# Attention and routed experts on one core: lead rows written ahead of the last load, two tiles' rows side by side, and two groups' norms on GpSimd

## Chip, core and metric

The kernel runs on one core of one Trainium2 chip. The metric is the device time of one execution in microseconds (us); for the kernel before the median of three runs is 536.72 us (535.98 to 536.99). About 0.2%, or 1.07 us, is what a measurement of this kernel can tell from no change. The engines are TensorE (PE, with weight loads as PEld), VectorE (DVE), ScalarE (ACT), GpSimd (POOL) and SyncE (SP), which here only issues DMAs.

## What is computed

There are 8 batches of 576 tokens with 8 heads of 64. Linear attention gives each token a 512-wide row, each head's part is normed by its root mean square, and each token goes to the one of 8 experts that its gate picks.

```python
kv  = einsum('bhsd,bhse->bhde', k, v)
out = einsum('bhsd,bhde->bhse', q, kv)
rms = sqrt(mean(out * out, -1) + 1e-6);  x = out / rms * g_norm      # (4608, 512)
logits = x @ w_gate;  e_idx = argmax(logits, 1)
y[mask e] = prob(e_idx) * sigmoid(x @ w_output_gate)[e] * relu(x @ w1[e]) @ w2[e]
```

## The kernel before

**First part, the rows.** The 4608 tokens are 36 tiles of 128. SP loads 54 pieces of 512 KB (`load`, L705): 32 of k and v (`kvm`), 4 remainders (`rem`) and 18 of q (`qT`), each of the latter for two tiles. The list `loads` holds them in a fixed order, and the last entry is `qT` piece 17, for tiles 34 and 35. A load needs a free slot out of `SLOTS - ROWS` = 20. For each tile `out_tile` (L788) does the PE matmuls into a PSUM tile `ops`, `out_rows` (L815) lets ACT copy the row (`xrow`), its squares (`sq`) and its gate products (`gp`), and `sums` (L833) lets DVE add up the squares (`ss`). ACT follows PE by one tile, and DVE follows ACT by one.

**Groups.** The tiles form groups of 16, 10 and 10. When a group's last `ss` is there, `route` (L849) turns its sums into inverse norms `rv` (nine DVE instructions, L858 to L872), scales the gate products, picks the expert, counts tokens per expert through small PE matmuls (`rp`), and closes the rows (`C_SCALE`, by a reciprocal). `STEPS` says after which tile which step of which group is written; `TAIL` is the order behind tile 35: `Q` flushes rows and sums, a digit is one step of that group, `W` loads W2, `C` is 8 matmuls of constants that keep PE at work, `L` is one step of the lead run, and so on. Rows go to DRAM (`xs`), where row 1 + 128 t + p is token p of tile t.

**Lead run.** The first 16 tiles' rows (group 0) are enough for a lead run of 256 tokens of the largest expert. Its rows are written by five DMAs (`xs<-xrow`, 8 tiles in one and 2 in each of four) as soon as the group is closed and no load is left (L1038). GpSimd then gathers the 256 rows by index (`gather(0)`, hook `G` at tile 35), DVE scales them by `rv` (`scale_heads`, L283), PE transposes them (`tps`, L307) and goes on with the lead's matmuls (L338, L590). The writes of groups 1 and 2 follow, then `gather(1)` for the rest of that expert's tokens, whose transposes stand in the lead's last matmuls, and after that the run of experts one behind another.

All four compute engines and SP take their work in the order in which it stands, one queue each. `qT`, `kvm`, `xs` and weight DMAs of SP share one hardware queue.

```python
if not loads and not opened[0]:                        # L1038: rows of the lead
    nc.sync.dma_start(out=xs[0:1, :].rearrange("o (a x) -> (o a) x", x=16), in_=zrow)
    open_rows(0)
...
xwrite(c0, xs[1 + c0 * P:1 + (c0 + k) * P].rearrange("(t p) x -> p t x", p=P), x)
```

Of the kernel before, what the change touches and what calls it, by code (L numbers as in the profile page):

```python
# [21 lines left out]
P = 128  # L22
# [78 lines left out]
def constants(gn, wg):
    k = np.zeros((P, K_N), np.float32)
    m = np.arange(P)
    e = np.arange(E)
    k[:, K_E:K_E + E] = e
    k[:, K_ER:K_ER + E] = e * NTOK
    k[:, K_SC:K_SC + E] = E - e
    k[:, K_CAP:K_CAP + E] = CAP
    k[:, K_FL:K_FL + E] = [c // P for c in CAP]
    k[:, K_TRI:K_TRI + E * E] = (e[None, :] < e[:, None]).reshape(-1)  # L110
    k[:, K_M1] = m + 1
    g = np.arange(NT)
    k[:, K_G:K_G + NT] = g
    k[:, K_V:K_V + NT] = g[None, :] * P + m[:, None] + 1
# [22 lines left out]
def body(ctx: ExitStack, tc: tile.TileContext, kvm, rem, qT, w1, w2, kc, xs, tab, out):  # L137
# [511 lines left out]
    wgs = cf[:, K_WG:K_N].rearrange("q (i x) -> q i x", i=2)  # L649
# [198 lines left out]

    def route(gi):  # L849

        ss, gp, lg = gst[gi]
        n = len(GROUPS[gi])
        last = gi + 1 == len(GROUPS)
        g0 = GROUPS[gi][0]
        vec = nc.vector

        a = sm.tile([P, GMAX, E], F32, name="ra", bufs=1)[:, :n]
        vec.tensor_scalar(out=a, in0=ss[:, :n], scalar1=1.0 / D, scalar2=1e-6, op0=ALU.mult, op1=ALU.add)  # L858
        y = sm.tile([P, GMAX, E], F32, name="ry", bufs=1)[:, :n]
        vec.tensor_scalar(out=y.bitcast(I32), in0=a.bitcast(I32), scalar1=-0.5,  # L860
                          scalar2=float(0x5F3759DF), op0=ALU.mult, op1=ALU.add)
        u = sm.tile([P, GMAX, E], F32, name="ru", bufs=1)[:, :n]
        rv = sm.tile([P, GMAX, E], F32, name="rv")[:, :n]

        q = 0.375 ** 0.5
        vec.scalar_tensor_tensor(out=u, in0=y, scalar=q, in1=y, op0=ALU.mult, op1=ALU.mult)
        vec.tensor_tensor(out=u, in0=u, in1=a, op=ALU.mult)
        vec.scalar_tensor_tensor(out=u, in0=u, scalar=-1.25 / q, in1=u, op0=ALU.add, op1=ALU.mult)
        vec.scalar_tensor_tensor(out=y, in0=u, scalar=1.875, in1=y, op0=ALU.add, op1=ALU.mult)
        vec.scalar_tensor_tensor(out=u, in0=y, scalar=-0.5, in1=y, op0=ALU.mult, op1=ALU.mult)  # L870
        vec.tensor_tensor(out=u, in0=u, in1=a, op=ALU.mult)
        vec.scalar_tensor_tensor(out=rv, in0=u, scalar=1.5, in1=y, op0=ALU.add, op1=ALU.mult)  # L872
# [91 lines left out]
        for t in range(n):  # L964
# [8 lines left out]
        vec.tensor_scalar(out=rc[:, :n, 0], in0=rc[:, :n, 1], scalar1=cf[:, K_M1:K_M1 + 1], scalar2=None, op0=ALU.mult)  # L973
# [146 lines left out]
    def rows_of_lead(out):  # L1120
# [262 lines left out]
    with ExitStack() as p3:  # L1383
# [4 lines left out]
        with tc.If(nreg > 0):  # L1388
            with tc.For_i(0, nreg) as i:
# [13 lines left out]
                nc.vector.tensor_copy(gi, gf)  # L1403
# [81 lines left out]
```

## Time and profile before

| what | us |
|---|---|
| median of 3 runs | 536.72 |
| the profiled execution's own time | 536.44 |
| its span | 534.6 |
| PE busy in the span | 522.6 |
| DVE, ACT, POOL busy | 382.3, 295.8, 265.4 |

The span is what the profiler saw between the first and the last instruction, the time also has what lies around it, here 1.84 us. PE is busy in nearly all of the span, but a share of busy time over the whole says little on one place: some of PE's work is constants that fill a wait. So the stretch that the change touches is read row by row: what each engine did there, what it waited for, and when DMAs landed.

### The profile page before, as it was taken

Reading aid. Unit: us, or ns where it says so; the run is one execution under the profiler, and the core shown is the slowest. Engines: PE = TensorE matmul, PEld = TensorE weight load, DVE = VectorE, ACT = ScalarE, POOL = GpSimd, SP = SyncE. Lnnn points to the kernel's source line nnn. Section 1 sums busy time; section 2 is a strip of 40 time slices with the busy share of each in tenths; the row PEclk is TensorE's granted clock in tenths of the full one; section 3 lists DMA queues with packets and bytes.
Section 4 is the critical chain, followed back from the end, with each engine's and each line's share of the span. In section 5 each row is a group of like instructions: output and inputs, shape, how many; then the busy total and the mean of one; then the engine's idle time right before and its main releaser. Section 6 shows DMA issues by size and latency. Waiting matters only on the chain.

```text
span 534.6 us, 10844 instructions
## 1 busy us (share of the span) xinstructions
PE 522.6 (98%) x4047; PEld 455.5 (85%) x4047; DVE 382.3 (72%) x834; ACT 295.8 (55%) x603; POOL 265.4 (50%) x275
## 2 busy tenths in 40 slices
PE   9899997999999999999999999999999999999995
PEld 6789886857988998899889988998899889889984
DVE  2225999974599779666895699578868978897710
ACT  1568673333558638365655565556465657485611
POOL 1000243232885269607960696079807963894011
PEclk9999999999999999999999999999999999999999
DMA  8999999965205340616044603360436053415001
GB/s 315 416 417 417 413 400 360 374 229 180 86 30 188 108 155 20 221 59 214 21 140 133 212 21 140 131 195 35 143 126 198 30 201 123 142 44 195 2 31 40
DMA packets 28420, 92.27 MB, mean 173 GB/s; under 512 B 3758, under 2 KB 3886, under 8 KB 28365
## 3 DMA queue, kind: packets, MB, share of 16 engines
q1 hardware_dynamic: 22124, 71.85, 36.5%
q0 software_dynamic: 6240, 19.70, 11.3%
q8 instruction: 33, 0.54, 0.4%
q14 instruction: 23, 0.18, 0.1%
HBM read 72.34 MB, written 19.64 MB: 172 GB/s over the span
## 4 chain that ended last, share of the span: by engine, by line
PE 78%; DMA 11%; DVE 8%; issue 1%; ACT 1%; POOL 0%; SPq 0%; POOLq 0%; ACTq 0%; DVEq 0%
PE yps L609 35%; PE hpsa L494 17%; PE hpsd L494 9%; DMA ld<-kvm 5%; PE hps L494 4%; PE hps L359 4%; PE yps L603 3%; DMA xs<-xrow 2%; DMA ld<-qT 2%; DVE ss L837 2%; PE tps L460 2%; DMA xg<-xs,gidx 2%; DVE gp L882 1%; DVE lg L886 1%; PE ops L811 1%
## 5 line engine op out<-in xcount | busy, mean ns | idle before, releaser
L609 PE MATMUL yps<-whi,hT 128*128 128x512 f32 (+3 forms) x560 | 184.2, 395 | 0.0
L609 PEld LDWEIGHTS yps<-whi,hT 128*128 128x128 f32 (+3 forms) x560 | 104.0, 186 | 22.3
L609 PE MATMUL yps<-wlo,hT 128*128 128x512 f32 (+3 forms) x280 | 109.7, 392 | 0.0
L623 POOL DMA_INDIRECT out<-y,oidx x41 | 51.8, 1263 | 89.1 <-ACT y L622 60.9
L265 POOL DMA_INDIRECT xg<-xs,gidx x42 | 43.9, 1046 | 93.9 <-ACT hT L514 37.9
L609 PEld LDWEIGHTS yps<-wlo,hT 128*128 128x128 f32 (+3 forms) x280 | 52.1, 186 | 9.9
L517 DVE SCALAR_TENSOR_TENSOR hT<-ct,hT 128x256 fp32r<-128x256 f32 (+9 forms) x88 | 44.0, 529 | 22.8 <-ACT hT L514 22.8
L514 ACT ACTIVATE hT<-ct 128x328 fp32r<-128x328 f32 (+13 forms) x56 | 34.6, 617 | 34.1 <-DVE ct L528 34.1
L494 PE MATMUL hpsa<-xb,wh 128*128 128x328 f32 (+6 forms) x224 | 47.5, 300 | 0.0
L494 PE MATMUL hpsd<-xT,wh 128*128 128x328 f32 (+6 forms) x224 | 47.4, 299 | 0.0
L494 PE MATMUL hpsa<-xT,wh 128*128 128x328 f32 (+6 forms) x224 | 47.4, 299 | 0.0
L837 DVE TENSOR_REDUCE ss<-sq 128x8 f32<-128x512 f32 x36 | 23.7, 680 | 29.3 <-ACT sq L827 29.3
L419 DVE SCALAR_TENSOR_TENSOR wl<-wraw,cf,wh 128x512 fp32r<-128x512 f32 (+1 forms) x56 | 44.0, 824 | 0.2 <-ACT wh L418 0.2
L283 POOL TENSOR_TENSOR xg<-xg 128x512 f32<-128x512 f32 (+7 forms) x36 | 38.3, 1075 | 11.2 <-DVE ct L549 9.0
L228 DVE TENSOR_TENSOR wlo<-wraw,whi 128x1024 fp32r<-128x1024 f32 x32 | 39.8, 1243 | 5.7 <-ACT whi L225 5.2
L419 DVE SCALAR_TENSOR_TENSOR wl<-ws,cf,wh 128x1024 fp32r<-128x1024 f32 x28 | 42.9, 1532 | 0.0
L622 ACT ACTIVATE y<-yps,tl 128x512 f32<-128x512 f32 (+3 forms) x37 | 25.4, 687 | 31.2 <-PE yps L609 17.7
L811 PE MATMUL ops<-aug,ld 64*128 64x80 f32 (+1 forms) x640 | 38.9, 271 | 1.5 <-ACT gp L828 1.4
L418 ACT ACTIVATE wh<-ws,cf 128x1024 fp32r<-128x1024 f32 x28 | 32.4, 1156 | 13.3 <-POOL ws L405 13.3
L494 PEld LDWEIGHTS hpsd<-xT,wh 128*128 128x128 f32 x224 | 37.1, 188 | 1.3
L494 PEld LDWEIGHTS hpsa<-xT,wh 128*128 128x128 f32 x224 | 37.0, 188 | 1.4
L494 PEld LDWEIGHTS hpsa<-xb,wh 128*128 128x128 f32 x224 | 37.1, 188 | 1.3
(231 smaller groups left out, 1145.3 us busy)
## 6 DMA issues: line engine op xcount, KB each, us to landing
wraw<-w SPq DMA_DIRECT2D x64, 512.0 KB, 4.0
ld<-kvm SPq DMA_DIRECT2D x32, 512.0 KB, 10.0
ld<-qT SPq DMA_DIRECT2D x18, 512.0 KB, 10.3
xs<-xrow SPq DMA_DIRECT2D x9, 528.0 KB, 6.7
xs<-xrow SPq DMA_DIRECT2D x2, 1320.0 KB, 11.3
xs<-xrow SPq DMA_DIRECT2D x1, 2112.0 KB, 12.4
ld<-rem SPq DMA_DIRECT2D x4, 512.0 KB, 9.8
xg<-xs,gidx POOLq DMA_INDIRECT x42, 3.9
```

The source lines that it names most:

```text
L228: eng.tensor_tensor(out=lo, in0=r, in1=hi.bitcast(F32), op=ALU.subtract)
L265: gathered = nc.gpsimd.indirect_dma_start(out=x[:M, :], out_offset=None, in_=rows, in_offset=bass.IndirectOffsetOnAxis(ap=gidx[:M, p, t:t ...
L283: return eng.tensor_tensor(out=v, in0=v, in1=f, op=ALU.mult)
L418: nc.scalar.activation(hi, x, AF.Copy, scale=gcol[:, 0:1])
L419: nc.vector.scalar_tensor_tensor(out=lo, in0=x, scalar=gcol[:, 0:1], in1=hi.bitcast(F32), op0=ALU.mult, op1=ALU.subtract)
L494: nc.tensor.matmul(ps, W[a][d], X[b][d], start=start and k == 0, stop=k == 5, skip_group_check=not start)
L514: S.activation(hh, x, AF.Relu)
L517: V.scalar_tensor_tensor(out=v(o, j1 - j0), in0=x[..., j0:j1], scalar=0.0, in1=hh[..., j0:j1].bitcast(F32), op0=ALU.max, op1=ALU.subtract)
L609: nc.tensor.matmul(ps[:M], a, b, start=(f == 0 and j == 0), stop=(f == 7 and j == 2))
L623: i_ = nc.gpsimd.indirect_dma_start(out=out, out_offset=bass.IndirectOffsetOnAxis(ap=oidx[:M, p, t:t + 1], axis=0), in_=y[:M], in_offset=N ...
L811: nc.tensor.matmul(v[r0:r0 + m, u, p, :], qt[g // 2][r, p, q0:q0 + m], augs[b % 3][r, p, :], start=True, stop=True)
L837: nc.vector.tensor_reduce(out=o, in_=sq, axis=AX.X, op=ALU.add)
```

## The change

Four things are changed.

1. `HELD = 1`: the last load stays back. The lead's writes are issued when the group is closed (`lead_known`) and only one load is left; that load follows them. `ROWS` is 10 and no longer 9, so that 19 slots are left for loads, and group 2's rows lie in pieces of 4, 4 and 2 tiles and no longer 5 and 5.
2. Rows of tiles 2j and 2j+1 lie side by side in DRAM: partition p of a write is one run of 4224 bytes and no longer two of 2112. Row numbers change with it (`2 * P` for `P`, two constants for m + 1), and `scatter_rows` has to undo it with six instructions where there were two.
3. For groups 0 and 1 the inverse norm is made tile by tile on GpSimd, with two instructions of 8 columns (scale and add, then `pow` -0.5); the nine DVE instructions stay for group 2 alone.
4. `TAIL` has four `C` ahead of the first `L`, and no longer seven.

```diff
-ROWS = 9
+ROWS = 10
-BIG = {26: 5, 31: 5}
+BIG = {26: 4, 30: 4}
-TAIL = "Q112WCCCCCCCLcL2L2L22L2L1L12L1KAL2AL"
+TAIL = "Q112WCCCCLcL2L2L22L2L1L12L1KAL2AL"
+HELD = 1
+NORM_GROUPS = 2
-        while loads and free and n:
+        while loads and free and n and (opened[0] or len(loads) > HELD):
 def sums():
         nc.vector.tensor_reduce(out=o, in_=sq, axis=AX.X, op=ALU.add)
+        if r is not None:
+            nc.gpsimd.tensor_scalar(out=o, in0=o, scalar1=1.0 / D, scalar2=1e-6, op0=ALU.mult, op1=ALU.add)
+            nc.gpsimd.tensor_tensor(out=r, in0=o, in1=cf[:, K_MH:K_N].to_broadcast([P, E]), op=ALU.pow)
 def route(gi):
+        if gi >= NORM_GROUPS:
...
-            xwrite(c0, xs[1 + c0 * P:1 + (c0 + k) * P].rearrange("(t p) x -> p t x", p=P), x)
+            xwrite(c0, xs[1 + c0 * P:1 + (c0 + k) * P].rearrange("(j p u) x -> p j (u x)", p=P, u=2), x)
...
-            if not loads and not opened[0]:
+            if len(loads) <= HELD and lead_known and not opened[0]:
                 nc.sync.dma_start(out=xs[0:1, :].rearrange("o (a x) -> (o a) x", x=16), in_=zrow)
                 open_rows(0)
+                load()
 def scatter_rows(q0, q1, t0, t1):
-        vec.scalar_tensor_tensor(out=oidx[:, q0:q1, t0:t1], in0=f, scalar=-1.0, in1=zf, op0=ALU.add, op1=ALU.add)
...
+        vec.tensor_tensor(out=a, in0=a, in1=b, op=ALU.bitwise_or)
+        vec.tensor_scalar(out=r, in0=r, scalar1=0xFFFF00, scalar2=None, op0=ALU.bitwise_and)
+        vec.tensor_tensor(out=oidx[:, q0:q1, t0:t1], in0=r, in1=a, op=ALU.bitwise_or)
```

On SP's queue, at the end of the loads, this stood (`ld` is a load, `xs` the rows in DRAM, `wraw` a weight):

```order
L712 DMA ld<-kvm 128x1024 x2
L712 DMA ld<-qT 128x1024 x2
L1039 DMA xs<-zrow 33x16
L1001 DMA xs<-xrow_110 128x8x528
L1001 DMA xs<-xrow 128x2x528 x4
L189 TENSOR_LOAD epos
```

and this stands now:

```order
L720 DMA ld<-kvm 128x1024 x2
L720 DMA ld<-qT 128x1024
L1056 DMA xs<-zrow 33x16
L1017 DMA xs<-xrow_110 128x4x1056
L1017 DMA xs<-xrow 128x1056 x4
L720 DMA ld<-qT 128x1024
L197 TENSOR_LOAD epos
```

One of the two `qT` loads has moved behind the five writes, whose rows are now runs of 1056 numbers.

On PE, at the last four tiles (32 to 35, a tile's eight matmuls in two rows), with buffer numbers and waits, this stood:

```order
L811 MATMUL ops_1407<-aug1_104,ld_881 128x80 [waits DMAHW5_49,PE_49]
L811 MATMUL ops_1407<-aug1_104,ld_881 128x80 x7
L811 MATMUL ops_1421<-aug1_104,ld_881 128x80 [waits PE_49,Activation_49]
L811 MATMUL ops_1421<-aug1_104,ld_881 128x80 x7
L811 MATMUL ops_1435<-aug1_104,ld_907 128x80 [waits DMAHW6_49,PE_49,Activation_49]
L811 MATMUL ops_1435<-aug1_104,ld_907 128x80 x7
L811 MATMUL ops_1454<-aug1_104,ld_907 128x80 [waits PE_49,Activation_49]
L811 MATMUL ops_1454<-aug1_104,ld_907 128x80 x7
```

and this stands now:

```order
L820 MATMUL ops_1445<-aug1_104,ld_932 128x80 [waits DMAHW5_49,PE_49]
L820 MATMUL ops_1445<-aug1_104,ld_932 128x80 x7
L820 MATMUL ops_1459<-aug1_104,ld_932 128x80 [waits PE_49,Activation_49]
L820 MATMUL ops_1459<-aug1_104,ld_932 128x80 x7
L820 MATMUL ops_1473<-aug1_104,ld_1176 128x80 [waits DMAHW4_49,PE_49,Activation_49]
L820 MATMUL ops_1473<-aug1_104,ld_1176 128x80 x7
L820 MATMUL ops_1492<-aug1_104,ld_1176 128x80 [waits PE_49,Activation_49]
L820 MATMUL ops_1492<-aug1_104,ld_1176 128x80 x7
```

The order of PE is the same, but the load that tile 34 reads (`ld_907`, now `ld_1176`) is the one that has moved.

On DVE, behind the last sum of group 0, this stood:

```order
L858 TENSOR_SCALAR ra<-ss 128x128
L860 TENSOR_SCALAR ry<-ra 128x128
L866 SCALAR_TENSOR_TENSOR ru<-ry 128x128
L867 TENSOR_TENSOR ru<-ru,ra 128x128
L868 SCALAR_TENSOR_TENSOR ru<-ru 128x128
L869 SCALAR_TENSOR_TENSOR ry<-ru,ry 128x128
L870 SCALAR_TENSOR_TENSOR ru<-ry 128x128
L871 TENSOR_TENSOR ru<-ru,ra 128x128
L872 SCALAR_TENSOR_TENSOR rv<-ru,ry 128x128
L837 TENSOR_REDUCE ss<-sq 128x8
L882 TENSOR_TENSOR gp_311<-gp_311,rv 128x2048
```

and this stands now:

```order
L896 TENSOR_TENSOR gp_311<-gp_311,rv 128x2048
L846 TENSOR_REDUCE ss<-sq 128x8
L900 TENSOR_REDUCE lg<-gp_311 128x256
L907 TENSOR_REDUCE mx<-lg 128x16
L909 TENSOR_TENSOR rd<-lg,mx 128x128
```

The nine instructions of the norm are gone from DVE there, and from group 1 in the same way; group 2 keeps them.

## Rows read from the trace of the kernel before

**Rows 1.** Page, busy us, share of the span and instructions of each engine.
```profile
PE 522.6 (98%) x4047; PEld 455.5 (85%) x4047; DVE 382.3 (72%) x834; ACT 295.8 (55%) x603; POOL 265.4 (50%) x275
```

**Rows 2.** Chain that ended last, 30 to 150 us: start, us, what.
```profile
88.09 4.40 DMA xg<-xs,gidx
...
100.68 12.77 DMA xs<-xrow
...
114.38 4.00 DMA xg<-xs,gidx
...
119.15 0.65 PE tps L307 x4
```

**Rows 3.** Timeline of SP, 60 to 81 us: start, us of issuing, what, count.
```profile
63.38 0.33 SPq L712 DMA_DIRECT2D ld<-qT  x1
...
67.59 7.67 SPq L1001 DMA_DIRECT2D xs<-xrow  x5
...
74.10 1.16 SPq L1001 DMA_DIRECT2D xs<-xrow  x1
76.71 3.76 SPq L198 DMA_DIRECT2D wraw<-w  x4
```

**Rows 4.** DMAs issued at 63.38, 74.10 and 76.71: KB, us to landing.
```profile
ld<-qT SPq DMA_DIRECT2D x1, 512.0 KB, 11.0
...
xs<-xrow SPq DMA_DIRECT2D x1, 528.0 KB, 11.5
...
wraw<-w SPq DMA_DIRECT2D x1, 512.0 KB, 10.0
```

**Rows 5.** Stretches: length, PE, PEld, DVE, ACT, POOL busy; PEclk, DMA share, GB/s.
```profile
20.00:40.00 20.00, 19.16 (x392) 16.97 (x391) 6.18 (x10) 14.49 (x37) 0.00 (x0) 1.00 1.03 417
75.00:82.00 7.00, 5.84 (x120) 5.24 (x116) 6.74 (x16) 5.12 (x14) 2.01 (x5) 1.00 1.06 383
...
532.00:533.00 1.00, 0.00 (x0) 0.00 (x0) 0.00 (x0) 0.00 (x0) 0.00 (x0) 0.63 0.23 86
533.00:534.00 1.00, 0.00 (x0) 0.00 (x0) 0.00 (x0) 0.00 (x0) 0.00 (x0) 0.50 0.00 0
```

**Rows 6.** Timeline of PE: start, us, line, operation, count, idle before.
```profile
1.17 5.64 PE L719 MATMUL kvp<-ones 128*128 128x256 bf16 x26 [1.17 <-DVE ones L662]
...
78.04 2.91 PE L811 MATMUL ops<-aug,ld 64*128 64x80 f32 x48
82.34 1.12 PE L811 MATMUL ops<-aug,ld 64*128 64x80 f32 x16 [1.39 <-ACT gp L828]
...
86.82 4.53 PE L719 MATMUL cps<-ones 128*128 128x256 bf16 x40 [0.17 <-ACT gp L828]
92.44 0.63 PE L307 MATMUL tps<-ident,xg 128*128 128x128 f32 x4 [1.09 <-DVE tl L303]
...
528.91 0.39 PE L609 MATMUL yps<-whi,hT 128*128 128x512 f32 x1
```

**Rows 7.** Timeline of DVE, same columns.
```profile
49.52 0.23 DVE L858 TENSOR_SCALAR ra<-ss 128x128 f32<-128x128 f32 x1
...
52.00 0.29 DVE L872 SCALAR_TENSOR_TENSOR rv<-ru,ry 128x128 f32<-128x128 f32 x1
...
86.17 1.27 DVE L837 TENSOR_REDUCE ss<-sq 128x8 f32<-128x512 f32 x2
...
91.60 0.74 DVE L283 TENSOR_TENSOR xg<-xg 128x512 f32<-128x512 f32 x1 [0.24 <-DMA xg<-xs,gidx]
```

**Rows 8.** Timeline of ACT, same columns.
```profile
84.14 0.65 ACT L825 COPY xrow<-ops 128x512 f32<-128x512 f32 x1
...
85.32 0.67 ACT L825 COPY xrow<-ops 128x512 f32<-128x512 f32 x1
85.86 0.63 ACT L827 ACTIVATE sq<-ops 128x512 f32<-128x512 f32 x1
```

**Rows 9.** Timeline of POOL, same columns.
```profile
52.36 2.92 POOL L874 COPY xrow<-rv 128x64 f32<-128x64 f32 x5 [44.15 <-DVE rv L872]
```

More of the change, by code (lines that the diff above doesn't have):

```diff
@@ L91 @@
 K_M1 = K_TRI + E * E
-K_G = K_M1 + 1
+K_G = K_M1 + 3
 K_V = K_G + NT
-K_C = K_V + NT
+K_C = K_V + 2 * NT
 K_I = K_C + E * TMAX
@@ L97 @@
 K_WG = K_GN + 1
-K_N = K_WG + 8 * E
+K_MH = K_WG + 8 * E
+K_N = K_MH + 1
 def constants(gn, wg):
@@ L110, in constants @@
     k[:, K_TRI:K_TRI + E * E] = (e[None, :] < e[:, None]).reshape(-1)
-    k[:, K_M1] = m + 1
+    k[:, K_M1:K_M1 + 3] = np.stack([m + 1, 2 * m + 1, 2 * m + 2], 1)
     g = np.arange(NT)
-    k[:, K_G:K_G + NT] = g
-    k[:, K_V:K_V + NT] = g[None, :] * P + m[:, None] + 1
+    k[:, K_G:K_G + NT] = g // 2
+    k[:, K_V:K_V + 2 * NT:2] = g[None, :] * P + m[:, None] + 1
+    k[:, K_V + 1:K_V + 2 * NT:2] = g[None, :] // 2 * (2 * P) + 2 * m[:, None] + g[None, :] % 2 + 1
     k[:, K_C:K_C + E * TMAX] = ((e[:, None] * NT + np.arange(TMAX)) * P).reshape(-1)
@@ L117, in constants @@
     k[:, K_GN:K_GN + 1] = gn
-    k[:, K_WG:K_N] = wg
+    k[:, K_WG:K_MH] = wg
+    k[:, K_MH] = -0.5
     return k
@@ L156, in body @@
     meti = cst.tile([P, NOVER], I32, name="meti")
-    cst.tile([P, 56], F32, name="pad")
+    cst.tile([P, 48], F32, name="pad")
     main = ctx.enter_context(ExitStack())
@@ L794, in out_tile @@
                        sm.tile([P, max(GR[gi % 2::2]), 16, H], F32, name=f"gp{gi % 2}", bufs=1),
-                       sm.tile([P, GMAX, 16], F32, name="lg"))
+                       sm.tile([P, GMAX, 16], F32, name="lg"),
+                       sm.tile([P, GMAX, E], F32, name="rv"))
         ps = ps_b.tile([P, 2, 512], F32, name="ops", tag="big")
@@ L820, in out_rows @@
         gi, t, n = group_of(g)
-        ss, gp, lg = gst[gi]
+        ss, gp, lg, rv = gst[gi]
         c0, k, x = next(c for c in chunks if c[0] <= g < c[0] + c[1])
@@ L828, in out_rows @@
         nc.scalar.copy(gp[:, t].rearrange("q x (u p) -> q u p x", u=2), v[:, :, :, D:W])
-        squares.append((sq, ss[:, t, :], gi if t + 1 == n else None))
+        squares.append((sq, ss[:, t, :], rv[:, t, :] if gi < NORM_GROUPS else None, gi if t + 1 == n else None))
     outs = []
@@ L834, in sums @@
     def sums():
-        sq, o, gi = squares.pop(0)
+        sq, o, r, gi = squares.pop(0)
         nc.vector.tensor_reduce(out=o, in_=sq, axis=AX.X, op=ALU.add)
+        if r is not None:
+            nc.gpsimd.tensor_scalar(out=o, in0=o, scalar1=1.0 / D, scalar2=1e-6, op0=ALU.mult, op1=ALU.add)
+            nc.gpsimd.tensor_tensor(out=r, in0=o, in1=cf[:, K_MH:K_N].to_broadcast([P, E]), op=ALU.pow)
         if gi is not None:
@@ L849, in route @@
     def route(gi):
-        ss, gp, lg = gst[gi]
+        ss, gp, lg, rv = gst[gi]
         n = len(GROUPS[gi])
@@ L855, in route @@
         vec = nc.vector
[L857 to L871, printed above, removed]
@@ L872, in route @@
-        vec.scalar_tensor_tensor(out=rv, in0=u, scalar=1.5, in1=y, op0=ALU.add, op1=ALU.mult)
+        rv = rv[:, :n]
+        if gi >= NORM_GROUPS:
+            a = sm.tile([P, GMAX, E], F32, name="ra", bufs=1)[:, :n]
+            vec.tensor_scalar(out=a, in0=ss[:, :n], scalar1=1.0 / D, scalar2=1e-6, op0=ALU.mult, op1=ALU.add)
+            y = sm.tile([P, GMAX, E], F32, name="ry", bufs=1)[:, :n]
+            vec.tensor_scalar(out=y.bitcast(I32), in0=a.bitcast(I32), scalar1=-0.5,
+                              scalar2=float(0x5F3759DF), op0=ALU.mult, op1=ALU.add)
+            u = sm.tile([P, GMAX, E], F32, name="ru", bufs=1)[:, :n]
+            q = 0.375 ** 0.5
+            vec.scalar_tensor_tensor(out=u, in0=y, scalar=q, in1=y, op0=ALU.mult, op1=ALU.mult)
+            vec.tensor_tensor(out=u, in0=u, in1=a, op=ALU.mult)
+            vec.scalar_tensor_tensor(out=u, in0=u, scalar=-1.25 / q, in1=u, op0=ALU.add, op1=ALU.mult)
+            vec.scalar_tensor_tensor(out=y, in0=u, scalar=1.875, in1=y, op0=ALU.add, op1=ALU.mult)
+            vec.scalar_tensor_tensor(out=u, in0=y, scalar=-0.5, in1=y, op0=ALU.mult, op1=ALU.mult)
+            vec.tensor_tensor(out=u, in0=u, in1=a, op=ALU.mult)
+            vec.scalar_tensor_tensor(out=rv, in0=u, scalar=1.5, in1=y, op0=ALU.add, op1=ALU.mult)
@@ L972, in route @@
                           in1=hk[:, :n].unsqueeze(2).to_broadcast(shp), op=ALU.is_equal)
-        vec.tensor_scalar(out=rc[:, :n, 0], in0=rc[:, :n, 1], scalar1=cf[:, K_M1:K_M1 + 1], scalar2=None, op0=ALU.mult)
+        for u in range(2):
+            vec.tensor_scalar(out=rc[:, u:n:2, 0], in0=rc[:, u:n:2, 1], scalar1=cf[:, K_M1 + 1 + u:K_M1 + 2 + u], scalar2=None,
+                              op0=ALU.mult)
         vec.tensor_tensor(out=rc[:, :n, 1], in0=rc[:, :n, 1], in1=gfull[:, g0:g0 + n], op=ALU.mult)
@@ L1125, in rows_of_lead @@
         vec.tensor_reduce(out=t5, in_=t4, axis=AX.X, op=ALU.add)
-        vec.scalar_tensor_tensor(out=out, in0=t5[:, 1], scalar=float(P), in1=t5[:, 0], op0=ALU.mult, op1=ALU.add)
+        vec.scalar_tensor_tensor(out=out, in0=t5[:, 1], scalar=float(2 * P), in1=t5[:, 0], op0=ALU.mult, op1=ALU.add)
     def scatter_rows(q0, q1, t0, t1):
-        f = gif[:, q0:q1, t0:t1]
-        zf = sm.tile([P, E, TMAX], F32, name="zf")[:, q0:q1, t0:t1]
-        vec.tensor_scalar(out=zf, in0=f, scalar1=0.0, scalar2=float(NTOK + 1), op0=ALU.is_equal, op1=ALU.mult)
-        vec.scalar_tensor_tensor(out=oidx[:, q0:q1, t0:t1], in0=f, scalar=-1.0, in1=zf, op0=ALU.add, op1=ALU.add)
+        r, a, b = (sm.tile([P, E, TMAX], I32, name=x, bufs=1)[:, q0:q1, t0:t1] for x in ("zr", "za", "zb"))
+        vec.tensor_scalar(out=r, in0=gif[:, q0:q1, t0:t1], scalar1=-1.0, scalar2=None, op0=ALU.add)
+        vec.tensor_scalar(out=a, in0=r, scalar1=1, scalar2=7, op0=ALU.bitwise_and, op1=ALU.logical_shift_left)
+        vec.tensor_scalar(out=b, in0=r, scalar1=254, scalar2=1, op0=ALU.bitwise_and, op1=ALU.logical_shift_right)
+        vec.tensor_tensor(out=a, in0=a, in1=b, op=ALU.bitwise_or)
+        vec.tensor_scalar(out=r, in0=r, scalar1=0xFFFF00, scalar2=None, op0=ALU.bitwise_and)
+        vec.tensor_tensor(out=oidx[:, q0:q1, t0:t1], in0=r, in1=a, op=ALU.bitwise_or)
     def ranks():
@@ L1398, in body @@
                     nc.vector.tensor_scalar(out=oh, in0=cf[:, K_I:K_I + P], scalar1=lo[:, g:g + 1], scalar2=None, op0=ALU.is_equal)
-                    nc.tensor.matmul(pi[:, 0:1], oh, cf[:, K_V + g:K_V + g + 1], start=(g == 0), stop=(g == NT - 1))
+                    nc.tensor.matmul(pi, oh, cf[:, K_V + 2 * g:K_V + 2 * g + 2], start=(g == 0), stop=(g == NT - 1))
                 gf = so.tile([P, 1], F32, name="ogf")
```

8 lines of the change are left out of this document (4 added, 4 removed).

## The prediction

> **What bounds the kernel now.** I read the page first: PE is busy for 98% of the span [rows 1], so time can only be won where PE waits or does work that serves nothing. Then the chain that ended last. It shows the one place that concerns this change: PE's constants up to 91.35, a gather at 88.09, scaling on DVE, and the first transposes of the lead run at 92.44 [rows 2, 6, 7]. From there PE has its work without a break: the second gather's transposes at 119.15 come just as PE reaches them [rows 2]. So the time of everything behind is fixed by when PE gets to its first `tps`, and the sum is about that start: **a lead start that moves by x us moves the end by x us.**
>
> What ends last before 92.44? Two things arrive almost together. The gather brings its rows at 91.6, and DVE waits 0.24 us for it [rows 7]; without that wait DVE would have been free at 91.36, since it works from `ss` of tiles 34 and 35 (ending at 87.44) through the closing of group 1 and the norms of group 2 without a pause. Both have to move for the lead to start earlier.
>
> Under this lies the DMA queue. Its share is 1.03 to 1.06 [rows 5], and what SP issues lands 10 to 11 us later [rows 4]. It is drained in order: the weight load issued at 76.71 lands at 86.7, behind the last lead write (issued 74.10, landed 85.6), although SP had issued it soon [rows 3, 4]. In that order the last `qT` load (63.38 + 11.0 = 74.4) is far ahead of its use at about 80 [rows 3, 4, 6].
>
> **The change, part by part.** *The last load behind the lead's writes.* Nothing is added or dropped in the queue by the swap, so what ended at 85.6 with the last lead write now ends with the load. The swap alone gives the lead writes one load's time: 0.52 MB at 417 GB/s, 1.25 us [rows 5].
>
> *Two rows in one run.* The 16 tiles are 4.33 MB. At the 383 GB/s of the stretch that wrote 2112-byte rows they take 11.3 us, at the 417 of 4096-byte loads 10.4 [rows 5]. No row shows a 4224-byte write; the loads are nearest in size, so I take 0.9 us off and keep 0 as the other end. Rows and page differ here. By the Trainium skill (DMA: Bandwidth & Descriptors, Specifications) runs of 512 bytes are already enough for the line rate, so pairing would bring nothing, and the load would land at 85.6 and not at 84.7.
>
> So the lead writes land at 85.6 - 1.25 - 0.9 = 83.5, and **the load for tiles 34 and 35 at 84.7** (84.7 to 85.6), 10.3 us later than before. Nothing earlier in the queue can hurry it, since the queue has been full from the start.
>
> *What waits for it.* PE's tiles 32 to 34 start at 78.04 and take 2.91 together [rows 6], so tiles 32 and 33 are done at about 80.0; then tile 34 waits, and in PE's order nothing else stands before it. PE is idle from 80.0 to 84.7. Behind tile 34 stand tile 35, the counting matmuls of group 1, the constants and the lead. ACT and DVE wait as well: DVE's queue has both sums, the closing of group 1 and the norms of group 2 ahead of the lead's scaling.
>
> *From the load to the lead.* A tile starts 1.05 after the one before and takes 1.12 [rows 6], at the full clock. ACT takes 1.18 from one tile to the next (84.14 to 85.32), and its squares are done 1.17 after the tile's copy starts (85.32 to 86.49) [rows 8]. Tile 34: PE 84.7 to 85.85. ACT's copy of tile 35 starts at 85.85 + 1.18 = 87.05, its squares end at 88.2, its `ss` at 88.85 (0.65 each) [rows 7]. In the kernel before that point was 87.44. From it to the scaling took 91.60 - 87.44, less the wait of 0.24, 3.92 us; nothing in it changes. The scaling starts at 92.8 and not at 91.6: **+1.2 us at the full clock.** The gather no longer matters: the second one started 2.5 us behind the last lead write's landing and took 4.40 [rows 2, 4], so now 83.5 + 2.5 + 4.4 = 90.4, which is 2.4 us before its use.
>
> *The clock in that wait.* At the end of the span PE stops at 529.3, and the granted clock is 0.63 in the stretch 532 to 533 and 0.50 behind it, the 1.2 GHz level [rows 5, 6]: it fell some 3 us after PE's last work. A wait of 4.7 us is longer than that. What the lower level costs: the same matmul of constants took 217 ns at the start of the span (5.64 us for 26), with PE just begun, and 113 ns (4.53 for 40) later [rows 6], a factor of 1.92; and there it took 5.6 us of work until they were fast. Tiles 34 and 35 would take 2.0 us each and no longer 1.05. PE then ends tile 35 at 84.7 + 2.0 + 2.1 = 88.8, ACT's squares 1.17 later at 90.0, `ss` at 90.65, and the scaling starts at 94.6: **+3.0 us.** The counting matmuls and four constants behind tile 35 end before that, even at half speed for a part.
>
> *The norms on GpSimd.* Group 0's nine instructions on DVE took from 49.52 to 52.29, 2.8 us [rows 7]; group 1's go too. What this frees on DVE lies ahead of the wait for the load and turns into idle time there. No row shows `pow`. A small instruction on POOL took 0.58 (2.92 for five) [rows 9], so I take a pair at 1.2, with DVE's 0.23 below; the pair of the last tile may take up to 2.8, the time of the nine, before the group's rows close later than now.
>
> *The rest.* Four more instructions in `scatter_rows` of the lead and one in each group's table, under 0.3 each [rows 7], stand on DVE ahead of tile 34's sum, where it now waits some 4 us: nothing; without that wait, 1.5 us. Eight more behind the lead's start stand beside PE's lead matmuls: nothing, up to 2.3 if that cover went. One slot fewer for loads costs nothing while SP waits for landings, at most one load's 1.25 us. Three constants fewer cost nothing: they filled a wait.
>
> *The second gather.* It waits for group 2's rows, which were issued at 100.68 and took 12.77 behind W2 [rows 2]. They come 3.0 us later, 103.7, behind a queue that has two W2 loads less to do there, so some 8 us and 112; before they landed at 113.45. PE wants them 3 us later. Covered by 4 us.
>
> **The rivals.** *(a) The clock holds.* Idle PE kept its clock for 1.39 us at 82.34 [rows 6], and how the fall stands to a wait of 4.7 us no row shows. Then +1.2 (to +2.1 where pairing gains nothing): 537.9.
>
> *(b) The load does not queue behind the writes, and the kernel is faster.* Were a read to pass waiting writes, it would land near 74.4 again. Then DVE has over 4 us less to do before the scaling, and the gather decides: 85.6 to 91.6 was 6.0, so 83.5 + 6.0 = 89.5, which is 2.1 us earlier: 534.6. The point from which it decides: the scaling starts 8.1 us behind the load at the full clock, so the end is earlier if the load lands before 83.5, and by over 0.2% before 82.4. Against it stands the weight load of 76.71, which did not pass [rows 3, 4].
>
> *(c) `pow` is slow.* If rv of tile 15 lags its sum by more than 2.8 us, the five writes are issued later than 67.59 [rows 3]; the queue runs dry at 74.4, so a lag of 10 us costs about 3 more, and the load with it: 543.
>
> *(d) The pairing gains nothing*, which is the upper end of each case: 0.9 more.
>
> **How the numbers follow.** The profiled execution took 536.44 for a span of 534.6; the median of the runs is 0.28 above it, and I add the differences to the median, 536.72. The likeliest case is the fallen clock, +3.0: **539.7** (chance 0.60, with part of the fall in it from 538.9 up, and 540.6 with d). (a) has 0.25, (b) 0.07, (c) 0.04, and 0.04 is left for what I don't see. 0.2% is 1.07 us, about what a measurement can tell from no change. Faster: (b) and some of what I don't see, 0.08. Within: the part of (a) in which the load lands a little before 84.7, 0.09. Slower: 0.83. The range goes from 537.5, under (a), to 540.9, over the likeliest with (d).
>
> **What would show it.** SP issues `qT` last behind five writes, and it lands at 84 to 86. PE has a gap of 4 to 5 us ahead of its tile 34, released by a DMA of `ld`, and a granted clock under 1.00 in it or just behind; tiles 34 and 35 take 2 us each. DVE is idle before the sum of tile 34, group 0's writes are issued no later than 67.6, and the first `tps` is at 95.4 (93.6 in a). The gather lands at 90 to 91 and is not waited for. PE's stretch from the first `tps` to the next expert is as long as before. I am wrong if the gap is not there, or if that stretch is shorter.

## The result, and the profile after

The changed kernel takes 542.35 us (median, 541.52 to 546.36) where the kernel before takes 536.54 beside it: a ratio of 1.0124, 95% interval 1.0081 to 1.0167. It is slower, as forecast, but by 5.8 us and not by 3.0, and above the range of 537.5 to 540.9.

The execution profiled first (546.36) had PE at the lower clock from about 20 to 30 us, which puts everything behind it some 3 us later; the rows of after therefore come from a second profile of the same kernel (541.86, after_again below).

The page's busy line, as in [rows 1]:

```profile
PE 523.5 (97%) x4023; PEld 456.0 (84%) x4023; DVE 380.3 (70%) x832; ACT 295.4 (55%) x603; POOL 316.2 (59%) x329
```

PE has 0.9 us more to do, in a span of 540.1 that is 5.5 longer. The engine that stands out is POOL: 50.8 us more. Its groups by line say on what (count, busy us, mean ns, idle before):

```profile
L850 POOL TENSOR_TENSOR rv<-ss,cf 128x8 f32<-128x8 f32 x26 | 42.7, 1643 | 2.2
L849 POOL TENSOR_SCALAR ss<-ss 128x8 f32<-128x8 f32 x26 | 5.3, 205 | 15.2 <-DVE ss L846 13.3
```

L850 is `pow`: 1.64 us for 8 columns. A pair takes 2.0 from start to start. The timeline of POOL (start, us, line, operation) shows what that does:

```profile
50.90 0.20 POOL L849 TENSOR_SCALAR ss<-ss 128x8 f32<-128x8 f32 x1
51.18 1.63 POOL L850 TENSOR_TENSOR rv<-ss,cf 128x8 f32<-128x8 f32 x1
52.77 2.84 POOL L888 COPY xrow<-rv 128x64 f32<-128x64 f32 x5
...
60.24 0.20 POOL L849 TENSOR_SCALAR ss<-ss 128x8 f32<-128x8 f32 x1 [0.63 <-DVE ss L846]
...
72.88 1.63 POOL L850 TENSOR_TENSOR rv<-ss,cf 128x8 f32<-128x8 f32 x1
74.51 4.67 POOL L982 TENSOR_SCALAR la<-ni,rlon 128x128 bf16<-128x128 f32 x8
79.26 0.20 POOL L849 TENSOR_SCALAR ss<-ss 128x8 f32<-128x8 f32 x1
79.54 1.66 POOL L850 TENSOR_TENSOR rv<-ss,cf 128x8 f32<-128x8 f32 x1
81.16 2.04 POOL L888 COPY xrow<-rv 128x16 f32<-128x16 f32 x5
```

Group 0's last pair ends at 52.81, half a microsecond behind the end of DVE's norms before [rows 7]. But from 60.24 POOL has no pause up to 83, and group 1's last pair (79.26) stands behind those of the tiles before it and behind `la`, POOL's share of the counting of group 0. DVE's timeline shows who waits for it:

```profile
71.49 1.87 DVE L846 TENSOR_REDUCE ss<-sq 128x8 f32<-128x512 f32 x3
81.24 1.49 DVE L896 TENSOR_TENSOR gp<-gp,rv 128x1280 f32<-128x1280 f32 x1 [7.88 <-POOL rv L850]
...
92.03 1.27 DVE L846 TENSOR_REDUCE ss<-sq 128x8 f32<-128x512 f32 x2
...
97.06 0.69 DVE L291 TENSOR_TENSOR xg<-xg 128x512 f32<-128x512 f32 x1
```

The sum of group 1's last tile is the first of the three at 71.49 (the other two belong to group 2) and is done at about 72.2; its `rv` is there at 81.2, 9.0 us behind it. DVE has its three sums done at 73.36 and stands still for 7.88 us. In the kernel before, DVE made these norms itself and then scaled group 1's gate products:

```profile
73.05 0.19 DVE L858 TENSOR_SCALAR ra<-ss 128x80 f32<-128x80 f32 x1
...
75.17 0.24 DVE L872 SCALAR_TENSOR_TENSOR rv<-ru,ry 128x80 f32<-128x80 f32 x1
...
75.92 1.50 DVE L882 TENSOR_TENSOR gp<-gp,rv 128x1280 f32<-128x1280 f32 x1
```

The scaling that was at 75.92 now starts at 81.24. From there DVE works without a pause up to the lead's scaling at 97.06, which was at 91.60 [rows 7]. PE's timeline:

```profile
79.38 2.02 PE L820 MATMUL ops<-aug,ld 64*128 64x80 f32 x32
85.27 2.00 PE L820 MATMUL ops<-aug,ld 64*128 64x80 f32 x16 [3.87 <-DMA ld<-qT]
87.64 2.00 PE L820 MATMUL ops<-aug,ld 64*128 64x80 f32 x16 [0.38 <-ACT gp L837]
...
90.27 4.72 PE L727 MATMUL cps<-ones 128*128 128x256 bf16 x32
97.84 0.63 PE L315 MATMUL tps<-ident,xg 128*128 128x128 f32 x4 [2.85 <-issue]
```

The wait for the held load is there as forecast: tile 34 starts at 85.27, at the lower clock. But DVE reaches that tile's sum only at 92.03, so it no longer matters. The first `tps` is 5.40 us later than in [rows 6], the span 5.5 longer.

Two executions among the experiments below, 554.01 us of pair_only and 553.36 of warm_c, took some 3% longer than the others of their kernel; they are in the medians of the table but not in its ratios.

### The profile page after: what moved, and what is told of

Its sections match the earlier page's. It is cut to its first block, busy times and chain, and to the rows that moved or that the text cites. A ratio compares the mean times of both kernels' runs of the same rounds, so it can differ in the third digit from the quotient of the medians.

```text
span 544.6 us, 10845 instructions
## 1 busy us (share of the span) xinstructions
PE 528.2 (97%) x4023; PEld 460.7 (85%) x4023; DVE 380.6 (70%) x832; ACT 296.0 (54%) x603; POOL 313.5 (58%) x329
## 4 chain that ended last, share of the span: by engine, by line
PE 85%; POOL 4%; DMA 4%; DVE 3%; issue 1%; ACT 1%; SPq 0%; POOLq 0%; another core or an unknown queue 0%; ACTq 0%
PE yps L617 35%; PE hpsa L502 17%; PE hpsd L502 8%; PE hps L502 4%; PE hps L367 3%; DMA ld<-kvm 3%; POOL rv L850 3%; PE yps L611 3%; PE hps L346 3%; PE yps L598 3%; PE ops L820 2%; PE tps L468 2%; PE kvp L744 2%; DVE ss L846 1%; POOL la L982 1%
## 5 line engine op out<-in xcount | busy, mean ns | idle before, releaser
L631 POOL DMA_INDIRECT out<-y,oidx x41 | 49.6, 1210 | 93.6 <-ACT y L630 65.0
L273 POOL DMA_INDIRECT xg<-xs,gidx x42 | 46.2, 1101 | 86.6 <-ACT hT L522 37.8
L820 PE MATMUL ops<-aug,ld 64*128 64x80 f32 (+1 forms) x640 | 43.5, 291 | 4.2 <-ACT gp L837 4.2
L427 DVE SCALAR_TENSOR_TENSOR wl<-wraw,cf,wh 128x512 fp32r<-128x512 f32 (+1 forms) x56 | 45.2, 846 | 0.2 <-ACT wh L426 0.2
L820 PEld LDWEIGHTS ops<-aug,ld 64*128 64x128 f32 (+1 forms) x640 | 37.6, 194 | 8.0 <-ACT gp L837 4.6
L850 POOL TENSOR_TENSOR rv<-ss,cf 128x8 f32<-128x8 f32 x26 | 42.7, 1643 | 2.2
```

The lines of the kernel that those rows point to most:

```text
L273: gathered = nc.gpsimd.indirect_dma_start(out=x[:M, :], out_offset=None, in_=rows, in_offset=bass.IndirectOffsetOnAxis(ap=gidx[:M, p, t:t ...
L427: nc.vector.scalar_tensor_tensor(out=lo, in0=x, scalar=gcol[:, 0:1], in1=hi.bitcast(F32), op0=ALU.mult, op1=ALU.subtract)
L631: i_ = nc.gpsimd.indirect_dma_start(out=out, out_offset=bass.IndirectOffsetOnAxis(ap=oidx[:M, p, t:t + 1], axis=0), in_=y[:M], in_offset=N ...
L850: nc.gpsimd.tensor_tensor(out=r, in0=o, in1=cf[:, K_MH:K_N].to_broadcast([P, E]), op=ALU.pow)
```

## Experiments

Two theories. **P**: `pow` backs POOL up, and group 1's `rv` sets the start of the lead. **L**: the held load, with PE's wait and fallen clock, makes nearly all of the loss. The column `before` is the median of the kernel before, timed beside each on the same chip; the ratio is to it, with its 95% interval.

| kernel | us, median | before | ratio, 95% | first `tps` | run behind the lead |
|---|---|---|---|---|---|
| the kernel before | | | | 92.44 | 124.99 |
| after_again | 542.30 | 536.65 | 1.0128 (1.0068 to 1.0188) | 97.84 | 130.10 |
| norm_dve | 540.23 | 536.85 | 1.0061 (1.0044 to 1.0078) | 95.44 | 127.70 |
| norm_only | 542.07 | 536.85 | 1.0092 (1.0075 to 1.0109) | 98.32 | 130.56 |
| unheld | 542.70 | 536.85 | 1.0124 (1.0078 to 1.0169) | 97.78 | 131.54 |
| pair_only | 537.57 | 536.85 | 1.0008 (0.9995 to 1.0020) | 93.46 | 125.69 |
| norm_g1 | 539.64 | 536.49 | 1.0054 (1.0037 to 1.0071) | 95.69 | 127.95 |
| pow_group | 566.14 | 536.49 | 1.0552 (1.0534 to 1.0569) | 122.05 | 154.32 |
| warm | 539.60 | 536.49 | 1.0050 (1.0034 to 1.0067) | 94.02 | 127.76 |
| warm_c | 539.27 | 536.65 | 1.0042 (1.0022 to 1.0063) | 97.79 | 130.05 |
| lead_first | 541.33 | 536.65 | 1.0078 (1.0050 to 1.0105) | 94.39 | 131.33 |
| held_only | 542.23 | 536.65 | 1.0099 (1.0068 to 1.0130) | 96.92 | 129.15 |

The last two columns are us of the profiled execution: PE's first `tps` and the first `hps` of the run of experts behind the lead. The profiles of warm_c and lead_first have the early stretch at the lower clock too: their tile 32 starts at 82.24 and 81.15 and not at 78.2, so with them the us from there are compared.

**The changed kernel once more (after_again).**

> The changed kernel once more, unaltered, for a profile of an execution near its median: the profiled one was 4 us above it, with PE at the lower clock from 19.4 to 29.7. If that early stretch belongs to single executions and not to the change, the others take 542 to 543 with the first transposes at 97.8 to 98.4, as in norm_only and unheld. If it belongs to the change, 545 to 546.

The median is 542.30 and the first `tps` at 97.84: the early stretch belongs to single executions, not to the change.

**The four parts, one left out or one alone.** norm_dve:

```diff
-NORM_GROUPS = 2
+NORM_GROUPS = 0
```

> The changed kernel with the norms of groups 0 and 1 back on DVE; the held load, the paired rows and the shorter tail stay. Theory P (the `pow` of GpSimd takes 1.64 us, a pair of it 2.0, the tiles come faster than that, and the queue that builds up holds back group 1 by 8 us): without it only the held load is left, as the prediction summed it, PE idle ahead of tile 34 and the first transposes at 93.6 to 95.4, so 538 to 540 us. Theory L (the held load and what it does to PE is nearly all of the loss, and `pow` hides behind the wait for it): 542, no better than the changed kernel.

It came as P had it, a little above the upper end (540.23, where 538 to 540 was expected). PE's timeline in norm_dve:

```profile
78.27 2.02 PE L820 MATMUL ops<-aug,ld 64*128 64x80 f32 x32
85.28 3.71 PE L820 MATMUL ops<-aug,ld 64*128 64x80 f32 x32 [5.00 <-DMA ld<-qT]
...
95.44 0.63 PE L315 MATMUL tps<-ident,xg 128*128 128x128 f32 x4 [0.90 <-issue]
95.91 0.82 PE L727 MATMUL kvp<-ones 128*128 128x256 bf16 x6
```

Two stretches of norm_dve (length, PE, PEld, DVE, ACT, POOL busy, PEclk, DMA share, GB/s):

```profile
80.00:85.00 5.00, 0.28 (x6) 0.13 (x4) 4.67 (x20) 2.15 (x6) 0.00 (x0) 0.71 1.03 414
85.00:90.00 5.00, 4.72 (x48) 4.48 (x49) 2.53 (x8) 2.39 (x7) 2.26 (x3) 0.50 1.03 419
```

PE waits 5.00 us for the held load, the granted clock falls to 0.50 (1.2 GHz), the last two tiles take 3.71, and the first `tps` comes at 95.44. The prediction's sum had 95.4.

norm_only is the kernel before with the norms alone:

```diff
+            nc.gpsimd.tensor_scalar(out=o, in0=o, scalar1=1.0 / D, scalar2=1e-6, op0=ALU.mult, op1=ALU.add)
+            nc.gpsimd.tensor_tensor(out=r, in0=o, in1=cf[:, K_MH:K_N].to_broadcast([P, E]), op=ALU.pow)
```

> The kernel before with only the norms of groups 0 and 1 on GpSimd, tile by tile; loads, rows and tail as before. P: POOL works without a break from about 36 us on, rv of group 1 comes at about 84 where DVE wanted it at about 76, the lead's first transposes come some 6 to 8 us later than at 92.44, and the time is 540 to 543. L: POOL's pairs hide, 536.5 to 537.5.

The norms alone cost 5.2 us, and the first `tps` is 5.88 later (6 to 8 was expected). DVE's timeline in norm_only:

```profile
71.51 1.87 DVE L842 TENSOR_REDUCE ss<-sq 128x8 f32<-128x512 f32 x3
81.83 1.49 DVE L892 TENSOR_TENSOR gp<-gp,rv 128x1280 f32<-128x1280 f32 x1 [8.45 <-POOL rv L846]
```

unheld is the changed kernel without the held load:

```diff
-HELD = 1
+HELD = 0
```

> The changed kernel with no load held back (the last load goes ahead of the lead's writes again); norms on GpSimd, paired rows and tail stay. P: 541 to 543, since POOL's queue sets the start of the lead with or without the load. L: 536 to 537.5, since the wait for the load is gone.

It gains nothing. Together the three say that the two losses don't add up: 3.4 us for the held load and 5.2 for the norms lie beside each other, and the later one, POOL's, is what the change costs. L falls.

pair_only leaves only the paired rows:

```diff
-HELD = 1
+HELD = 0
-NORM_GROUPS = 2
+NORM_GROUPS = 0
-TAIL = "Q112WCCCCLcL2L2L22L2L1L12L1KAL2AL"
+TAIL = "Q112WCCCCCCCLcL2L2L22L2L1L12L1KAL2AL"
```

> Of the change only the paired rows (with ten row slots and pieces of 4, 4 and 2 tiles) are left: norms on DVE, no load held, seven C in the tail. The lead's writes land at most 0.9 us earlier and the gather then at most 0.24 us before DVE wants it: 536.3 to 536.8 in both theories. If it is over 537.5, the pairing or the extra instructions of the scatter indices cost something that neither theory has.

Its median is 0.07 above the bound set there, but the interval holds 1: no loss and no gain is shown. Its profile has two things that speak against a gain. The four more instructions of `scatter_rows` put DVE's last sums 0.6 us later (86.17 in [rows 7]):

```profile
86.78 1.27 DVE L846 TENSOR_REDUCE ss<-sq 128x8 f32<-128x512 f32 x2
```

And PE's timeline shows a fallen clock: 56 constants in 8.60 us, where 40 took 4.53 [rows 6].

```profile
82.40 1.49 PE L820 MATMUL ops<-aug,ld 64*128 64x80 f32 x16 [1.27 <-ACT gp L837]
...
85.02 8.60 PE L727 MATMUL cps<-ones 128*128 128x256 bf16 x56 [0.39 <-ACT gp L837]
93.46 0.60 PE L315 MATMUL tps<-ident,xg 128*128 128x128 f32 x4
```

In the kernel before PE waited 1.39 us at the same place and kept its clock [rows 6]. The fall is not in every execution: seven were granted a mean clock of 0.991 or 0.992 over the whole and took 537.07 to 538.07 us; two, at 0.998 and 1.000, took 536.98 and 536.84, as the kernel before. So what pair_only loses goes with the fallen clock.

**Which group it is.** norm_g1:

```diff
-NORM_GROUPS = 2
+NORM_GROUPS = 1
```

> The changed kernel with GpSimd's norms for group 0 alone; group 1 has them on DVE again. P as the traces have it (the loss comes from group 1's rv, which DVE waits 8 us for; that of group 0 is late by under 1 us): 539.8 to 540.6, as norm_dve. The prediction's rival c (it is group 0's late rows, which put off the lead's writes and with them the held load): 541.5 to 543.

With `pow` for group 0 alone the time is that of norm_dve (539.64, just under the 539.8 to 540.6 expected): what `pow` costs is all group 1's. SP's timeline of the changed kernel (start, us of issuing, what, count) agrees: the lead's writes are not late (67.59 in [rows 3]):

```profile
67.32 4.19 SPq L1017 DMA_DIRECT2D xs<-xrow  x5
71.98 0.62 SPq L720 DMA_DIRECT2D ld<-qT  x1
```

**What `pow` costs.** pow_mult:

```diff
-op=ALU.pow)
+op=ALU.mult)
```

> The changed kernel with a multiplication in place of `pow` in GpSimd's tensor instruction, nothing else (the inverse norm is thus left out of what is computed: the gate products and rows are scaled wrongly, and the numbers of tokens per expert can differ a little). P in its narrow form (`pow` itself is the slow part): the instruction falls from 1.64 to about 0.3 us, POOL keeps up, what is left is the held load as in norm_dve, some 540 us. Rival (two small instructions per tile on POOL are too much in any form, by their waits and their place ahead of other work): 542 to 543 as before. Token counts can move the time of the expert runs, so the first transposes (95 to 96, or 98) tell it apart, not the end alone.

It leaves out the inverse norm, so the gates see other numbers and tokens can go to other experts; its 687 us therefore tell nothing, but its start does. The first `tps` is at 95.31, as in norm_dve, and the instruction in the same place, with the same operands, costs an eighth, as POOL's groups by line say:

```profile
L850 POOL TENSOR_TENSOR rv<-ss,cf 128x8 f32<-128x8 f32 x26 | 5.3, 204 | 2.2
```

So `pow` is the slow part. DVE's work beside it is not: in the changed kernel `pow` took 1.66 us at 79.54, while DVE stood still, and 1.63 at 60.52, while DVE worked.

pow_group has one pair for a whole group, behind its last sum:

```diff
+                o, r = gst[gi][0][:, :n], gst[gi][3][:, :n]
...
+                nc.gpsimd.tensor_tensor(out=r, in0=o, in1=cf[:, K_MH:K_N].unsqueeze(1).to_broadcast([P, n, E]), op=ALU.pow)
```

> The changed kernel with one pair of GpSimd instructions for a whole group, behind its last sum, in place of one pair for each tile: `pow` over 128 and over 80 columns. It asks what the 1.64 us are made of. If they are a fixed cost for each instruction, a group's pair takes 2 to 3 us, POOL has no queue, and the time is that of norm_dve, about 540. If they go with the columns (0.2 us each), the pair of group 0 takes 26 us and that of group 1 16 us, the lead's writes come over 20 us late, and the time is over 555.

POOL's timeline in pow_group:

```profile
49.93 20.77 POOL L852 TENSOR_TENSOR rv<-ss,cf 128x128 f32<-128x128 f32 x1
...
92.29 13.13 POOL L852 TENSOR_TENSOR rv<-ss,cf 128x80 f32<-128x80 f32 x1
```

20.77 us for 128 columns and 13.13 for 80 are (20.77 - 13.13) / 48 = 0.16 us a column and 0.4 besides, which gives 1.67 for 8, where 1.64 was measured: the cost goes with the columns. Most of it is work and not the price of starting an instruction. One pair for group 1 takes 13.5 us where ten take 20, but the whole group has to wait for it.

**What the clock costs.** warm is norm_dve with constants in PE's wait:

```diff
-HOOKS = {35: "G"}
+HOOKS = {34: "ccccccc", 35: "G"}
```

> norm_dve with 42 matmuls of constants (4.7 us at the full clock) on PE between tile 33 and tile 34, in the gap of 5.0 us in which PE waits for the held load. If the fallen clock is what makes the +1.2 us of the held load into +3.0, as the prediction had it, tiles 34 and 35 take 2.2 us and not 3.7, the first transposes come at 93.6 to 94.0 and not at 95.4, and the time is 538.0 to 538.6. If the clock costs nothing there, 540.2 as norm_dve. If the constants delay tile 34, over 540.5.

PE's timeline in warm:

```profile
80.17 4.76 PE L727 MATMUL kvp<-ones 128*128 128x256 bf16 x42
85.24 2.02 PE L820 MATMUL ops<-aug,ld 64*128 64x80 f32 x32 [0.31 <-ACT gp L837]
...
94.02 1.09 PE L315 MATMUL tps<-ident,xg 128*128 128x128 f32 x4 [2.77 <-DVE tl L311]
94.90 1.49 PE L727 MATMUL kvp<-ones 128*128 128x256 bf16 x6
```

The two tiles take 2.02 and no longer 3.71, and the first `tps` is 1.42 earlier. But the four C, now at full clock, end early; PE idles 2.77 us, the clock falls there instead (six constants take 1.49, where norm_dve's take 0.82), and the run behind the lead starts when it did in norm_dve. The time, 539.60, misses the 538.0 to 538.6 that was expected. warm_c fills that wait too:

```diff
-TAIL = "Q112WCCCCLcL2L2L22L2L1L12L1KAL2AL"
+TAIL = "Q112WCCCCCCLcL2L2L22L2L1L12L1KAL2AL"
```

> warm with six C behind tile 35 where it has four. In warm the first transposes came at 94.02, 1.4 us earlier than in norm_dve, but PE had stood idle for 2.77 us just before and then ran at the lower clock to about 98, and only 0.6 us were left of it. If that second fall is what took the rest, then with PE kept at work up to the transposes they come at 94.0 again, at full clock, and the time is 538.2 to 538.8 (+1.6 to +2.2 on the kernel before). If the rest went somewhere else, 539.4 to 539.8, as warm.

The median, 539.27 (538.87 without the execution of 553.36), is above what was expected, and five of its executions lie at 538.66 to 538.87, at the edge of it. In its profile the first `tps` comes 15.55 us behind the start of tile 32 (norm_dve 17.17, the kernel before 14.40). There the load was not waited for any more, since PE came to tile 32 some 4 us late and the constants ended last; in warm, where the load landed at about 85.1, just ahead of tile 34, the stretch is 15.80. So with the clock held the load costs 1.2 to 1.4 us up to the first `tps`, near the prediction's rival (a), and the clock 1.4 to 1.6. The times say less: the five executions were granted a mean clock of 0.997 to 0.999, like the kernel before (mostly 0.994 to 1.000), and are still 2.0 to 2.2 us above its median, and the interval (1.0022 to 1.0063) doesn't part warm_c from warm. So the clock's share in the 3.0 us is shown in the rows; how much of it filler gives back in the end, and where the rest goes behind the first `tps`, stays open.

**Undoing the order.** lead_first, from warm, scales the lead's rows ahead of group 1's closing and group 2's norms:

```diff
-TAIL = "Q112WCCCCLcL2L2L22L2L1L12L1KAL2AL"
+TAIL = "QCCCLcL112W2L2L22L2L1L12L1KAL2AL"
```

> warm with DVE's order turned round: the lead's two scalings come straight behind the sum of tile 35, ahead of group 1's closing and group 2's norms (3.8 us of DVE that the lead doesn't need), and three C before them. In norm_dve the gathers were issued at 85.1 and 86.6 and in the kernel before they took 4.4 to 5.0 us, so the lead's rows are there at 90.0 and 91.0. If DVE's order is then the last thing that holds the lead, the first transposes come at 90.6 to 91.2 where the kernel before has 92.44, and the time is 535.0 to 536.0, faster than both kernels. If what was put behind (group 1's rows in DRAM 1.6 us later, W2 behind them) is waited for at the second gather or in the lead's matmuls, 537 to 540.

From tile 32 to the first `tps` it needs 13.24 us, 1.2 less than the kernel before. From there to the next run it needs 36.94 and not 32.55. PE's timeline:

```profile
104.34 0.41 PE L937 MATMUL mrp<-ohb,ones 128*128 128x80 bf16 x10 [2.52 <-DVE ohb L919]
104.62 0.20 PE L939 MATMUL mrp<-ohb,triu 128*128 128x88 bf16 x1
104.66 7.10 PE L346 MATMUL hps<-xT,wraw 128*128 128x256 f32 x24
```

What was put behind is waited for: group 2's `ohb` stops PE for 2.52 us, and the 24 matmuls behind it take 7.10, at a granted clock of 0.63 from 104 to 108, where they took 5.41 before. Both expected cases were missed: 541.33 is above 535 to 536 and above 537 to 540. The fall of the clock can't be all of it: the other five executions were granted a mean clock of 0.995 to 0.999 and took 540.59 to 541.35; how their loss divides is not shown. Whether the counting can be moved behind more of the lead's matmuls was not tried; no version here beats the kernel before.

**What the pairing brings.** held_only is the kernel before with the last load put behind the writes:

```diff
-        while loads and free and n:
+        while loads and free and n and (opened[0] or len(loads) > HELD):
...
-            if not loads and not opened[0]:
+            if len(loads) <= HELD and lead_known and not opened[0]:
...
+                load()
```

> The kernel before with only its last load put behind the five lead writes (rows of 2112 bytes, norms on DVE, nine row slots and seven C as before). Beside norm_dve, which has the pairing too, it prices the pairing: by the 0.9 us that the prediction took for it, the load lands 0.9 us later than in norm_dve (PE's tile 34 starts at 86.2 where that has 85.28), the first transposes come at 96.3, and the time is 541. If the pairing gains nothing, tile 34 starts at 85.3 and the time is 540.2, or a little less since PE has three C more to keep its clock.

PE's timeline in held_only:

```profile
85.57 3.71 PE L813 MATMUL ops<-aug,ld 64*128 64x80 f32 x32 [5.51 <-DMA ld<-qT]
...
89.83 7.25 PE L721 MATMUL cps<-ones 128*128 128x256 bf16 x56
96.92 0.60 PE L309 MATMUL tps<-ident,xg 128*128 128x128 f32 x4
```

The load lands 0.29 us later than with pairs in norm_dve (85.28), a third of the 0.9 taken. Single executions differ by as much, though: norm_g1, with pairs too, has its tile 34 at 85.53. What the pairs do change clearly is the rate: between 75 and 82 us the DMAs move 384 GB/s in held_only and 383 in the kernel before [rows 5], and 398 in norm_dve and 399 in norm_g1. For the 4.33 MB that is, by an estimate, 0.4 us. The rest of held_only's later start is the constants: seven C, the first of them at the lower clock (0.50 to about 92), last till 97.1, and the lead starts behind them, 1.48 later than behind norm_dve's four. What was expected for it, the load 0.9 later and so 96.3, comes close to 96.92 by another way, and by luck. The time, 542.23, is above the 541 expected.

## Why the prediction was wrong

**The step that failed is the price of the norms on GpSimd.** It took a pair at 1.2 us from the row of five copies [rows 9], in which nothing is like `pow`, and it weighed the delay of one pair (2.8 us of slack at a group's end), so that the norms entered the sum at nothing. Two things were wrong there. The pair takes 2.0. And 26 pairs are not 26 single delays but a queue, with the copies (2.84) and `la` (4.67) in it: POOL had no pause from 60.24 on, and the last pair of group 1 ended 9.0 us behind its sum. Of these, 4.75 are `la`, which stands ahead of that pair (74.51 to 79.26); by an estimate from these rows, with the pair ahead of `la`, `rv` would have come at 76.4, half a microsecond behind the 75.92 at which it was used before. That order was not tried. By the Trainium skill (GPSIMD Engine Reference, Performance versus the Vector engine) elementwise work of two tensors needs about 2.6 cycles an element at 1.2 GHz, by an estimate 2 ns for a column of 128 partitions. The 160 ns measured here are far from it: the page's rule holds no price for `pow`.

**"What this frees on DVE lies ahead of the wait for the load" failed with it.** DVE lost the nine instructions of norms ahead of group 1's scaling (2.4 us, 73.05 to 75.41 in the kernel before) and got a wait of 7.88 in their place. The scaling starts 5.3 us later than it did, and that is the 5.40 of the first `tps`.

**Rival (c) came near the time, 543, but not the way.** It had group 0's norms late and with them the writes and the load. Group 0's last `rv` lagged its sum by 3.2 us (49.64 to 52.81), just past its bound of 2.8, but the writes went out at 67.32, no later than before; norm_g1 shows that group 0's norms cost nothing. Its chance of 0.04 was too low since no row bounded `pow` from above.

**That the end moves with the start of the lead held.** From the profiles, the first `tps` and the span are later by 3.00 and 3.2 (norm_dve), 5.88 and 5.8 (norm_only), 4.48 and 4.6 (held_only), 5.40 and 5.5 (after_again). It doesn't hold where the part behind the start changes too, as in warm, lead_first and unheld (5.34 and 6.8).

**The held load was summed right.** As the forecast without the norms, norm_dve has what it says: tile 34 at 85.28 (84.7 to 85.6), the clock at 0.50, the two tiles at 3.71 (4.1), the first `tps` at 95.44 (95.4), the time at 540.23 beside 536.85, 3.4 more (3.0). That 95.4 was met so closely is in part luck: the load landed 0.6 later than 84.7, and the two tiles took 0.4 less. The factor of 1.92 came from constants at the start of the span, where the profile gives a granted clock of 1.00 (0 to 6 us), so those rows did not show the lower level; norm_dve and warm do, with 3.71 for the two tiles at 0.50 and 2.02 at 1.00. The gather was not waited for. In the changed kernel this is hidden: its DVE comes to tile 34 too late for the load to matter.

**The pairing was over-sized**: 0.04 to 0.29 us by the landing (norm_g1, norm_dve), 0.4 by the rate, and not 0.9. It took the rate of the loads, 417 GB/s, for the paired rows, which went at 398. Had its end of 0 been taken, the sum would have been 0.3 off on the other side. By the Trainium skill (DMA: Bandwidth & Descriptors, Specifications) runs of 512 bytes already reach the line rate; the measured gain is nearer to that than to the prediction's term, but by the rate it is not nothing.

**Three C fewer** cost nothing, as said, and the reason was half of it: with the load held, PE comes to them so late that the seven would themselves have held the lead, as held_only shows. There they started at 89.83; at the full clock (113 ns each, from [rows 6]) they would by an estimate still have ended at 96.2, behind DVE's first scaled rows (95.64).

## What to carry to other kernels

An operation that no row of the trace shows has no price; before work is moved to an idle engine, its rate (instructions by duration against the pace at which the work comes) counts more than the delay of one of them, and so does what else stands in that engine's queue. Two waits that lie beside each other don't add: leaving out each part in turn shows which ends last, and a part that costs 3.4 us alone can cost nothing in the whole. Filler that keeps an engine's clock up is itself work, and when it starts late, the more so at the lower clock, it becomes the wait.

## What the runs showed of the hardware

GpSimd's `pow` took 1.64 us for 8 columns of 128 partitions, 13.13 for 80 and 20.77 for 128, where a multiplication with the same operands took 0.20 for 8. PE's granted clock fell in or just behind waits of quite different length: 5.00 us in norm_dve, 2.77 in warm and 1.27 in pair_only, while it held through 1.39 in the kernel before and through 2.85 in the changed kernel (1.00 from 95 to 100). So the length of the one wait doesn't decide it; what does is open.
